# Four transposes in a row between two writes, and two neighbours exchanged on VectorE: a fused convolution and gated-MLP kernel

## The chip, the cores and the metric

The kernel runs on one core of a Trainium2 chip. The metric is the device time of one execution in microseconds (us). The kernel before took 234.76 us, the median of three runs (234.39 to 234.94). Besides these there is one profiled execution, from which all rows of the trace come; its own time is in the table below.

The engines are named as the profile names them: PE is TensorE (PEld its weight loads), DVE is VectorE, ACT is ScalarE, POOL is GpSimd, SP is SyncE. SP computes nothing; it issues DMAs, in order, and "SPq" is its queue.

## What is computed

Two branches work on the same normalised input and are added to it. Sequence length is 2048, width 640, inner width of the MLP 1728, all in bf16.

```python
x = A_q
xn = _layernorm(x, axis=-1)
return x + _A_ref(xn, A_k, A_v, A_shift_k, A_ssm_k, A_ssm_D) + _B_ref(xn, B_w_gate, B_w_up, B_w_down)
```

Branch A shifts `A_k` with four taps per channel, multiplies by `A_v` (the product is called kv), convolves kv along the sequence with the long filter `A_ssm_k` (by Fourier transforms of double length), adds `kv * ssm_D`, and multiplies by xn. Branch B is a gated MLP:

```python
g = jnp.einsum("bsd,df->bsf", x, w_gate)
u = jnp.einsum("bsd,df->bsf", x, w_up)
h = _sigmoid(g) * u
return jnp.einsum("bsf,fd->bsd", h, w_down)
```

## The kernel before, in words

**Tiling.** A sequence row r is held as r = 16 p + b: p is the partition (128 of them), b one of 16 blocks. Branch B works on four groups t = 0 to 3 of four blocks each, that is 512 rows; branch A on five chunks c = 0 to 4 of 128 channels.

**Branch B, for each group.** DVE computes the statistics of x and the normalised rows (ln_norms, L210 and L214; ln_xn, L227), POOL the reciprocal root (ln_pow, L222). The products need xn transposed. For group 0 PE does that. For groups 1 to 3 a transposing DMA per block does it, called a turn: xn_turn(g, i), L249, issued on SP's queue, 128 x 640 elements each. Then come 13 gate products and 13 up products of five matmuls each (gate_mm and up_mm, both L270) and one mixed product for the last 64 columns (both_mm, L291). ACT takes the sigmoid of a gate product out of PSUM (gate_ev, L279). DVE multiplies it with the up product (up_ev, L285), which frees that PSUM slot; this is called a gate product below. Then PE forms the down products (down_mm, L314), in two halves of the width, and DVE adds them to x (down_ev, L319); this is an eviction.

**Branch A, for each chunk.** DVE forms kv in 16 operations (kv_op, L347 to L356) and brings the filter into the same layout with 32x32 transposes (h_turn, L333). The Fourier transform is done in two stages of matmuls with a trip through DRAM between them. Stage 1 has eight groups (st1_mm, L373 and L375); each is copied out of PSUM (st1_ev, L231 on ACT, L234 where it is on DVE), and two copies at a time are written to DRAM (wr1(c, k), L391, 512 KB, issued on SP). rd2 (L408) reads them back reordered, st2_mm (L417) is stage 2, st2_ev copies it out, and prod multiplies with the filter's spectrum in two steps on DVE: a shuffle of 32 partitions (L430) and a product (L432). Two inverse stages follow (inv1_mm, L446; inv2_mm, L487), again with a write (wr2) and a read (rdb) between them. inv1_ev copies out of PSUM, inv2_q (L492) multiplies with xn, inv2_x (L497) adds to x.

**PSUM.** There are two pools. One, with two places, serves the stages of branch A; the other, with four, serves all products of branch B and inv2. A matmul that takes a place waits until the engine that last read it is done. The tile framework, not the kernel, hands out places, and sets all waits from the order in which the program issues its steps.

**Order.** The loops only fill lists: each kind of step has a letter and a list of its calls. A string, ORDER (L660 to L670), then names the next step to issue, letter by letter, for all engines at once. Within one engine the order of the letters is the order of execution; between engines only the waits count. The letters that the change touches: `e` is a turn, `w` a wr1, `u` an up_ev, both_mul or down_ev, `p` a prod, `H` an h_turn. The letters that stand near them: `g` a product of branch B on PE, `a` and `A` a group of stage 1 and its copy, `s` a gate_ev, `l` ln_norms or ln_xn, `P` ln_pow, `k` a kv_op.

**Around the first place of the change.** While PE still forms group 0's down products, interleaved with stage 1 of chunk 0, DVE normalises group 1. SP's queue has loaded chunk 1's filter and v. In the kernel before it then holds turn 0, turn 1, wr1(0, 0), wr1(0, 1), turn 2, turn 3 of group 1, and behind them the loads for chunk 2 (halo, taps, k), the other two writes of chunk 0 and the load of x's third group (L135). The first gate product of group 1 reads all four turned blocks.

**Around the other two.** Some 60 us later PE works on group 2's products and stage 1 of chunk 3, while DVE evicts the last down product of group 1 and runs ahead with chunk 4's kv and with prod of the groups of stage 2.

Of the kernel before, what the change touches and what calls it, by code (L numbers as in the profile page):

```python
# [57 lines left out]
def kernel(  # L58
# [600 lines left out]

    ORDER = """  # L660
    mmmZmmmmmmmmmTmmmmmmmggsguggsggsuukkgggssukkggukksukkkgsgukkgggsgukkkggsgsukkguHstggguHDmmmsukkkkggg
    ukgukgaAlugaAlPgaAlllueewgaAwlPgaAklleeHDkgaAugaAkKTwgaAukkKwgaAukkHgaAukkkggsgggnustgaukKKgghakAsul
    rwAsakggluglsaksAugHggkAVrubkkkBlswKBukgggaTVsgpkusukawgDkHPlngAaAaskgAKwAkukgskpbgtkBsllBugauAkgagp
    sAaguswVpakAguhkHHAgrgDkwcgVklguCkkraeCagAgkAbuBkuBkkggKgkbBKpggBaeualwukkggeIuurlTklAehrgwtVbBBggag
    kAagppswuAagkuaKswrgpAAkaHAskWgHupDgakuVsAggswucglJukkgkrCsbgpBugaBaAgAWkkgsbspugPkrBgwpgsRnFkukgprc
    wgCJusgbgusgpuBdBWppbqrgsdBlRuqgBcqlCggJbsggksuBupgllkBbBgrqkWBgeaaeAAuppwdgaduRegaIAgrugpaAqaeqggup
    AwcCqpJguugdbgFBgbBqqgugBppdcpWCuJqgrpsgqbgBsuwFgrgqsbuBgpBRsuWgpdcpqqdguJgqCsrrbFBgsgRbugBBpdrsppug
    cdCqugCqgbsgWBqpqggusrBRbpudgrgqWspBpBqcupdJsgCbgRBpgBqqguWgsppuqscCudgJsguqgqgRdWgoquuqoddRgggRqquq
# [37 lines left out]
```

## Time and profile before

| | |
|---|---|
| median of three runs | 234.76 us (234.39 to 234.94) |
| the profiled execution's own time | 235.41 us |
| its span, first to last instruction | 233.6 us |
| PE busy | 228.1 us |
| DVE busy | 203.8 us |
| ACT busy | 122.0 us |
| DMA | 56.79 MB, mean 243 GB/s |

How to read the rows: in a timeline a row has its start and duration in us from the span's start, the engine, the line of the kernel, the operation, what it writes and reads, and how many instructions are merged in it. A bracket at the end gives the idle time of the engine just before the row and what ended it. A row of SPq is the issue of a DMA, that is, the time in which the queue was occupied with it; its data moves later, and "DMA to landing" counts from the start of the issue to the moment when all data has arrived. The duration of a matmul's row is modelled and longer than the distance to the next one, as matmuls are pipelined. A row of the view by windows gives, for a stretch of time, its length, the busy time of PE, PEld, DVE, ACT and POOL, the TensorE clock that was granted (1.00 is full speed), and in the last two columns the busy share of the 16 DMA engines and the GB/s that they moved.

### The profile page before, as it was taken

How to read it: one execution, taken by the hardware profiler on the slowest of the kernel's cores; microseconds unless marked ns; L12 is line 12 of the kernel's file. 1: busy time of each engine (PE TensorE's matmuls, PEld its weight loads, DVE VectorE, ACT ScalarE, POOL GpSimd, SP SyncE). 2: the span in 40 equal slices, each digit the busy share in tenths (PEclk: the TensorE clock that was granted, in tenths of full speed). 3: DMA queues.
4: the chain of work that ended last, by engine and by line, in shares of the span. 5: the costliest groups of instructions: out<-in, count | busy, mean ns of one | idle time of the engine just before them, and what ended most of it. 6: DMA issues, size and time to landing. Idle time of an engine off the chain costs nothing.

```text
span 233.6 us, 5418 instructions
## 1 busy us (share of the span) xinstructions
PE 228.1 (98%) x2199; PEld 130.9 (56%) x2200; DVE 203.8 (87%) x359; ACT 122.0 (52%) x156; POOL 12.0 (5%) x24
## 2 busy tenths in 40 slices
PE   7999999998999999999999999999999999999995
PEld 2854446786454555677554444478653544446772
DVE  5446999889679999999999999997899999897773
ACT  2533222376264877766775837674556667762000
POOL 5210000021001100000011000000000000000000
PEclk9999999999999999999999999999999999999999
DMA  6999999999899899999999899589989999464874
GB/s 198 327 278 221 248 282 361 203 96 262 268 260 289 213 389 244 276 213 232 320 273 263 219 340 278 161 206 173 286 216 311 269 267 250 126 149 128 232 253 143
DMA packets 93803, 56.79 MB, mean 243 GB/s; under 512 B 50964, under 2 KB 87890, under 8 KB 93650
## 3 DMA queue, kind: packets, MB, share of 16 engines
q1 hardware_dynamic: 93346, 56.03, 92.4%
q10 hardware_dynamic: 432, 0.41, 0.6%
q8 instruction: 17, 0.28, 0.5%
q14 instruction: 8, 0.07, 0.1%
HBM read 36.12 MB, written 18.35 MB: 233 GB/s over the span
## 4 chain that ended last, share of the span: by engine, by line
PE 91%; DVE 6%; DMA 1%; POOL 0%; issue 0%; ACT 0%; DVEq 0%
PE pu L270 24%; PE pg L270 23%; PE pd L314 22%; PE psb L487 4%; PE ps L417 3%; PE ps L375 3%; PE ps L373 3%; PE psa L446 2%; PE idle L513 2%; PE pg L291 2%; DVE st L210 1%; DVE x L319 1%; DMA xnT<-xn 1%; PE pg L261 1%; PE pu L261 1%; PE pt L241 1%
## 5 line engine op out<-in xcount | busy, mean ns | idle before, releaser
L270 PEld LDWEIGHTS <-w 128*128 128x128 bf16 x500 | 46.6, 98 | 55.8 <-issue 5.9
L314 PE MATMUL pd<-wd,hT 128*128 128x320 bf16 (+2 forms) x447 | 66.1, 299 | 0.1
L270 PE MATMUL pg<-xnT,w 128*128 128x512 bf16 x250 | 62.2, 379 | 1.1 <-DMA xnT<-xn 1.1
L270 PE MATMUL pu<-xnT,w 128*128 128x512 bf16 x250 | 62.2, 379 | 0.3 <-DVE hT L285 0.3
L314 PEld LDWEIGHTS <-hT 128*128 128x128 bf16 x448 | 41.7, 98 | 18.1 <-issue 2.4
L279 ACT ACTIVATE sig<-pg 128x512 bf16<-128x512 f32 x52 | 31.1, 601 | 32.3 <-PE pg L270 26.9
L285 DVE TENSOR_TENSOR hT<-sig,pu 128x512 bf16<-128x512 bf16 x52 | 34.9, 678 | 10.5 <-PE pu L270 5.2
L231 ACT CAST xz<-ps 128x1024 bf16<-128x1024 f32 x36 | 35.1, 1015 | 15.8 <-PE ps L417 15.7
L231 ACT CAST t<-ps 128x1024 bf16<-128x1024 f32 x24 | 23.9, 1013 | 19.9 <-PE ps L375 16.7
L432 DVE TENSOR_TENSOR xz<-xz 128x2048 bf16<-128x2048 bf16 x20 | 24.4, 1220 | 0.2
L375 PE MATMUL ps<-kvh,S1t 128*128 128x128 bf16 x160 | 21.7, 220 | 0.0
L373 PE MATMUL ps<-kvh,S1t 128*128 128x128 bf16 x160 | 21.6, 218 | 0.0
L351 DVE TENSOR_TENSOR tmp<-kx,sc 128x1024 bf16<-128x1024 bf16 x30 | 20.5, 683 | 0.3
L353 DVE TENSOR_TENSOR acc<-acc,tmp 128x1024 bf16<-128x1024 bf16 x30 | 20.4, 681 | 0.3
L319 DVE TENSOR_TENSOR x<-pd,x 128x320 bf16<-128x320 f32 (+2 forms) x32 | 15.1, 479 | 4.3 <-PE pd L314 4.1
L373 PEld LDWEIGHTS <-S1t 128*128 128x128 bf16 x160 | 15.5, 97 | 2.7 <-DVE kvh L356 0.2
L375 PEld LDWEIGHTS <-S1t 128*128 128x128 bf16 x160 | 15.4, 96 | 2.5
L210 DVE BATCH_NORM_STATS2 st<-x 128x6 f32<-128x320 bf16 x32 | 13.9, 476 | 2.2 <-DMA x<-in_A_q_dram 2.2
L231 ACT CAST TBt<-ps 128x1024 bf16<-128x1024 f32 x14 | 13.9, 1013 | 2.9 <-PE ps L375 2.9
L492 DVE TENSOR_TENSOR yx<-psb,xn 128x512 bf16<-128x512 f32 x20 | 13.7, 686 | 1.4 <-PE psb L487 0.8
L430 DVE STREAM_SHUFFLE xz<-xz 128x512 f32<-128x512 f32 x20 | 14.5, 725 | 0.0
L231 ACT CAST ao<-psa 128x1024 bf16<-128x1024 f32 x9 | 9.0, 1013 | 8.3 <-PE psa L446 6.9
(53 smaller groups left out, 157.8 us busy)
## 6 DMA issues: line engine op xcount, KB each, us to landing
t<-d SPq DMA_DIRECT2D x15, 512.0 KB, 5.9
d<-t SPq DMA_DIRECT2D x13, 512.0 KB, 5.7
d<-TBt SPq DMA_DIRECT2D x7, 512.0 KB, 6.4
d<-ao SPq DMA_DIRECT2D x6, 512.0 KB, 4.7
bi<-d SPq DMA_DIRECT2D x6, 512.0 KB, 4.5
kvh<-in_A_v_dram SPq DMA_DIRECT2D x10, 256.0 KB, 6.3
hn<-in_A_ssm_k_dram SPq DMA_DIRECT2D x20, 128.0 KB, 7.2
S1t<-d SPq DMA_DIRECT2D x4, 512.0 KB, 7.0
```

Source lines behind the costliest of these rows:

```text
L210: nc.vector.bn_stats(st[:, i, SD * s2:SD * s2 + SD], x[:, b, s2 * 320:(s2 + 1) * 320])
L231: nc.scalar.copy(out=out, in_=in_)
L270: nc.tensor.matmul(pg[:, :], lhsT=w[:, c, u * UP + fc * P:u * UP + (fc + 1) * P], rhs=xnT[:, :, c, :], start=(c == 0), stop=(c == NC - 1))
L279: nc.scalar.activation(sig[fc][:, :], pgs[0, fc][:, :], ACT.Sigmoid)
L285: nc.vector.tensor_tensor(hT[:, fc, :], sig[fc][:, :], pgs[1, fc][:, :], ALU.mult)
L314: nc.tensor.matmul(pd[:, :], lhsT=hT[:, fc, bb * P:(bb + 1) * P], rhs=wd[:, fc, es], start=(fc == 0), stop=(fc == NFC - 1))
L319: nc.vector.tensor_tensor(x[:, 4 * t + bb, es], pds[bb, half][:, :], x[:, 4 * t + bb, es], ALU.add)
L351: nc.vector.tensor_tensor(d["tmp"][:, :, :], kx[:, lo + 3 - m:hi + 3 - m, :], sb(m), ALU.mult)
L353: nc.vector.tensor_tensor(d["acc"][:, :, :], d["acc"][:, :, :], d["tmp"][:, :, :], ALU.add)
L373: nc.tensor.matmul(ps[:, i, 0:P], lhsT=S1[:, h, b, :], rhs=cin[c]["kvh"][:, 0, b, :], start=True, stop=True)
L375: nc.tensor.matmul(ps[:, i, P:2 * P], lhsT=S1[:, h, b, :], rhs=hp[:, b // 2, b % 2, :], start=True, stop=True)
L432: nc.vector.tensor_tensor(z[:, 1:3, :, :], z[:, 0:1, :, :].to_broadcast((P, 2, 8, P)), z[:, 1:3, :, :], ALU.mult)
```

## The change

Only the order string differs. No step is added, removed or altered.

```diff
-    ukgukgaAlugaAlPgaAlllueewgaAwlPgaAklleeHDkgaAugaAkKTwgaAukkKwgaAukkHgaAukkkggsgggnustgaukKKgghakAsul
+    ukgukgaAlugaAwlPgaAlllueegaAlPgaAklleewHDkgaAugaAkKTwgaAukkKwgaAukkHgaAukkkggsgggnustgaukKKgghakAsul
...
-    kAagppswuAagkuaKswrgpAAkaHAskWgHupDgakuVsAggswucglJukkgkrCsbgpBugaBaAgAWkkgsbspugPkrBgwpgsRnFkukgprc
+    kAagpupswAagkuaKswrgpAAkaHAskWguHpDgakuVsAggswucglJukkgkrCsbgpBugaBaAgAWkkgsbspugPkrBgwpgsRnFkukgprc
```

Read engine by engine, it does this:

- On SP's queue, wr1(0, 0) moves ahead of turns 0 and 1 of group 1, and wr1(0, 1) behind turns 2 and 3. The queue then holds wr1(0, 0), turn 0, turn 1, turn 2, turn 3, wr1(0, 1). What stands before and behind these six is unchanged.
- On DVE, down_ev(1, 3, 1), the last eviction of group 1, moves ahead of prod(3, 0), the shuffle of stage 2's group 3.
- On DVE, up_ev(2, 1), the second gate product of group 2, moves ahead of h_turn(4, 1), the second 32x32 transpose of chunk 4's filter.
- The orders on PE, ACT and POOL are the same.

## The prediction, made before the result was known

> **What bounds the kernel now.** I began with the busy times and the chain of work that ended last.
>
> ```profile
> PE 228.1 (98%) x2199; PEld 130.9 (56%) x2200; DVE 203.8 (87%) x359; ACT 122.0 (52%) x156; POOL 12.0 (5%) x24
> PE 91%; DVE 6%; DMA 1%; POOL 0%; issue 0%; ACT 0%; DVEq 0%
> ```
>
> TensorE (PE) is the bound: 98% of the span, 91% of the chain. Order alone can only remove moments in which PE stands still. The list of waits names two behind the first microseconds; PE's timeline shows them in brackets. As the ends of matmul rows are modelled, I measure a stop from start to start. The undisturbed step from a stage-1 matmul to a product is 0.06 us:
>
> ```profile
> 119.08 0.22 PE L375 MATMUL ps<-kvh,S1t 128*128 128x128 bf16 x1
> 119.14 0.59 PE L270 MATMUL pg<-xnT,w 128*128 128x512 bf16 x2
> ```
>
> The first stop, at the first gate product of the second group, costs 58.22 - 56.89 - 0.06 = **1.27 us**:
>
> ```profile
> 56.89 0.22 PE L375 MATMUL ps<-kvh,S1t 128*128 128x128 bf16 x1
> 58.22 1.24 PE L270 MATMUL pg<-xnT,w 128*128 128x512 bf16 x5 [1.12 <-DMA xnT<-xn]
> ```
>
> The second, at up_mm(2,1), has no bracket and costs 0.21 - 0.06 = **0.15**:
>
> ```profile
> 117.40 0.22 PE L375 MATMUL ps<-kvh,S1t 128*128 128x128 bf16 x1
> 117.61 1.24 PE L270 MATMUL pu<-xnT,w 128*128 128x512 bf16 x5
> ```
>
> The third, at up_mm(2,3), costs 0.50 - 0.06 = **0.44**:
>
> ```profile
> 123.22 0.22 PE L375 MATMUL ps<-kvh,S1t 128*128 128x128 bf16 x1
> 123.72 1.24 PE L270 MATMUL pu<-xnT,w 128*128 128x512 bf16 x5 [0.27 <-DVE hT L285]
> ```
>
> Together 1.86 us: the most that this change can win, as it removes no work.
>
> The first stop is a wait for the last transpose of x's second group (xn_turn(1,3)). Those transposes are issued on SyncE's queue:
>
> ```profile
> 41.37 1.34 SPq L183 DMA_DIRECT2D kvh<-in_A_v_dram  x1
> 48.17 1.31 SPq L249 DMA_TRANSPOSE xnT<-xn  x1
> 49.60 2.21 SPq L249 DMA_TRANSPOSE xnT<-xn  x1
> 51.91 0.53 SPq L391 DMA_DIRECT2D d<-t  x1
> 52.54 0.37 SPq L391 DMA_DIRECT2D d<-t  x1
> 53.00 2.31 SPq L249 DMA_TRANSPOSE xnT<-xn  x1
> 55.41 1.24 SPq L249 DMA_TRANSPOSE xnT<-xn  x1
> 56.70 0.57 SPq L165 DMA_DIRECT2D kx<-in_A_k_dram  x1
> ```
>
> The queue stands from 42.71 (41.37 + 1.34) to 48.17, the first turn waiting for its xn. Then two turns, both writes of stage 1 (wr1) and two more turns fill it without a gap to 56.65. The last turn lands 2.7 us after its issue began, the row below, so at 58.11, and PE starts at 58.22.
>
> ```profile
> DMA to landing us min/median/max: 2.7/2.7/2.7
> ```
>
> The other two stops are PSUM slots that VectorE (DVE) frees too late:
>
> ```profile
> 116.46 0.72 DVE L430 STREAM_SHUFFLE xz<-xz 128x512 f32<-128x512 f32 x1
> 117.08 0.47 DVE L319 TENSOR_TENSOR x<-pd,x 128x320 bf16<-128x320 f32 x1
> 117.48 0.68 DVE L351 TENSOR_TENSOR tmp<-kx,sc 128x1024 bf16<-128x1024 bf16 x1
> ```
>
> The eviction (L319) ends at 117.55 and PE starts at 117.61.
>
> ```profile
> 122.01 1.09 DVE L333 STREAM_TRANSPOSE kvh<-hn 128x512 f32<-128x512 f32 x1
> 123.03 0.63 DVE L285 TENSOR_TENSOR hT<-sig,pu 128x512 bf16<-128x512 bf16 x1
> 123.60 0.72 DVE L430 STREAM_SHUFFLE xz<-xz 128x512 f32<-128x512 f32 x1
> ```
>
> The gate product (L285) ends at 123.66 and PE starts at 123.72. In both places the change exchanges just the first two of these three rows.
>
> **Part 1, the queue.** Nothing is added or removed: six DMAs change order. The first write needs the second eviction of stage 1:
>
> ```profile
> 45.92 1.01 ACT L231 CAST t<-ps 128x1024 bf16<-128x1024 f32 x1 [0.39 <-PE ps L375]
> ```
>
> That ends at 46.93, so the write issues at about 47.0 for some 0.5 us, inside the queue's standing time. The first two turns keep their places. The third and fourth need these rows of xn:
>
> ```profile
> 50.98 0.80 DVE L227 TENSOR_SCALAR xn<-x,mv,rstd 128x640 bf16<-128x640 bf16 x2 [0.59 <-POOL rstd L222]
> ```
>
> Both are ready by 51.78, the first of them earlier, so the third turn starts at 51.87 instead of 53.00. With the four durations of the rows (1.31, 2.21, 2.31, 1.24) the last one is issued by 55.52 and lands, at 58.11 - 56.65 = 1.46 after its issue, at 56.98; with 1.3 for the third, which then has only a turn ahead of it, at 55.97. PE needs it by about 56.84. So the first stop goes, or all but about 0.15: I take 1.2 of the 1.27; the bounds are 1.27 and, by the second rival below, a loss.
>
> Behind them the second write goes out at 55.57 instead of 52.54. Its landing took 4.1 us there, and its buffer is filled again by chunk 1's third eviction:
>
> ```profile
> DMA to landing us min/median/max: 4.1/4.1/4.1
> ```
> ```profile
> 65.39 1.01 ACT L231 CAST t<-ps 128x1024 bf16<-128x1024 f32 x1 [2.60 <-issue]
> ```
>
> That would be 59.7 against 64.1 (65.39 less the 1.27): nobody waits. If the cover went, ACT would wait, and PE for its bank. The next load (chunk 2's halo, 56.70) then starts at 56.15, 0.55 us sooner, or up to 2.0 sooner if all turns take 1.25.
>
> **Part 2, what is late next.** PE alone being early isn't enough, since its PSUM slots come from DVE, and DVE waits for loads:
>
> ```profile
> 67.79 0.89 DVE L210 BATCH_NORM_STATS2 st<-x 128x6 f32<-128x320 bf16 x2 [0.16 <-DMA x<-in_A_q_dram]
> ```
> ```profile
> 78.59 0.63 DVE L285 TENSOR_TENSOR hT<-sig,pu 128x512 bf16<-128x512 bf16 x1
> ```
> ```profile
> 79.30 1.24 PE L270 MATMUL pu<-xnT,w 128*128 128x512 bf16 x5
> ```
>
> From 67.79 on DVE runs practically without a gap, and its start there is pinned by the load of x's third group. At 79.30 PE takes a slot that DVE freed at 79.22. So behind this point PE keeps only as much of its gain as DVE has moved, and DVE moves only as much as that load lands sooner. How much is that? The DMA engines by windows:
>
> ```profile
> 51.00:52.00 1.00, 1.00 (x14) 0.82 (x12) 1.00 (x3) 0.61 (x2) 0.00 (x0) 1.00 0.06 6
> 54.00:55.00 1.00, 1.00 (x13) 0.77 (x11) 1.00 (x3) 0.66 (x1) 0.00 (x0) 1.00 1.03 397
> 56.00:57.00 1.00, 1.00 (x13) 0.78 (x11) 1.00 (x3) 0.80 (x1) 0.00 (x0) 1.00 1.01 207
> 57.00:60.00 3.00, 1.88 (x11) 0.86 (x10) 2.93 (x6) 1.51 (x2) 0.00 (x0) 1.00 0.54 124
> ```
>
> The last two columns are DMA share and GB/s. From 57 to 60 they are idle for 0.46 of 3 us, 1.4 us, because the queue hands out too little; another 0.94 us is lost at 51, while the queue still issues turn 1 and next to nothing moves. With the queue ahead by 0.55 to 2.0 us and a write (512 KB, 1.3 us at 397 GB/s) to fill the hole at 57, the load lands sooner by between 0.55 (the issue alone) and about 1.9 (nearly all idle time used). I take **1.0**, nearer the lower end, as the row that is sure is the issue's. So of the first stop 1.0 us survives at 79.30.
>
> **Part 3, the exchanges on DVE.** At 117 the eviction no longer stands behind the shuffle (0.62 us from start to start), at 123 the product no longer behind the 32x32 transpose (1.02). Both stops, 0.15 and 0.44, are shorter, so both go. What moves back, a shuffle by 0.40 us (117.48 less 117.08, the eviction's step) and a 32x32 transpose by 0.57, costs nothing by these rows: behind each pair every row of DVE starts when it did, and the shuffle's reader and chunk 4's h are wanted only there or later. If PE took its slot from DVE without a stop here, the exchanges would be worth nothing. PE would then be 1.0 + 0.59 us ahead, DVE only 1.0, and DVE gets no faster. The tightest later place is this one:
>
> ```profile
> 149.65 1.22 DVE L234 CAST ao<-psa 128x1024 bf16<-128x1024 f32 x1
> ```
> ```profile
> 151.13 0.43 PE L417 MATMUL ps<-t,SMt 32*32 32x512 bf16 x16
> ```
>
> PE takes the bank at 151.13 and DVE left it at 150.87. The slack is 0.26, less the 0.06 of every hand-over, so 0.2 of the lead on DVE can be kept: 1.0 + 0.2 = **1.2 us** in all. Behind that DVE is the one that waits for PE, as in this row, so the lead stays to the end.
>
> ```profile
> 159.69 1.22 DVE L234 CAST t<-ps 128x1024 bf16<-128x1024 f32 x1 [1.24 <-PE ps L375]
> ```
>
> The sum: the profiled execution took 235.41 us (span 233.6 and 1.8 around it), 0.65 above the median of the runs, and becomes 234.2. The median, 234.76, becomes **233.5**.
>
> One page can be held against the way I priced the turns. In the window at 56, which holds little but two turns, the engines move 207 GB/s, against 397 at 54, where the write moves. The Trainium skill (Advanced Engine Details and Errata, X-Bar Transpose) says that transposing DMAs on trn2 are as fast as regular ones, at an expected 350 to 400 GB/s. The trace disagrees by nearly a factor of two. By the page a turn's 164 KB would take an estimated 0.41 us, and the sum would be that of the fourth rival below.
>
> **The rivals.**
> - *DVE stays where it is.* If the load of x lands no sooner, DVE is pinned at 67.79, PE is stopped at 79.30 for what it won at 58, and only the 0.2 us of slack at 151 is left from the exchanges, with 0.05 from 79.30. For it: at 54 and 56 the share is 1.0, so what lands late may be set by the engines and not by the issue. Against it: the 1.4 us of idle time just before. 234.76 - 0.25 = **234.5**.
> - *The turns pace each other: slower.* Turn 1, right behind turn 0, took 2.21 us to issue; turn 3, right behind turn 2, only 1.24. If a turn in a row costs 2.3, four end at 48.17 + 9.2 + 0.15 = 57.5, the last lands at 59.0 (PE +0.9), and the halo starts at 58.15 instead of 56.70. The load of x and with it DVE are 1.4 late, PE at 79.30 too; 0.2 comes back from the exchanges: 234.76 + 1.2 = **236.0**. It decides from a mean of 1.93 us a turn, at which the halo keeps its 56.70; in the rows the mean is 1.77. Against it: the long ones also had a stalled engine or two writes ahead of them.
> - *The exchanges do nothing.* Which of four PSUM slots a product gets is the tile framework's choice in program order, and with the order changed it may pick another. Then 0.2 is lost: **233.7**.
> - *The turns run at the rate of a plain write.* With four issues of 1.25 the halo goes out at 54.65, DVE moves by all that PE feeds it (1.27, and the 0.16 it waited at 67.79), and PE keeps 1.43 + 0.2: 234.76 - 1.63 = **233.1**. For it: the two short rows. Against it: the 207 GB/s.
>
> **How the numbers follow.** The forecast gets 0.59, the plain-write rival 0.08, the idle exchanges 0.10, the pinned DVE 0.13, the pacing turns 0.10. A measurement can tell 0.2%, 0.47 us, from no change. Faster by more than that are the first three, 0.77; the same is the pinned DVE, 0.13; slower the pacing turns, 0.10. The range goes from all three stops gone (234.76 - 1.86 = 232.9) to just above the pinned DVE (234.6) and leaves out the slower rival.
>
> **What would show it.** Right: the first write issued at about 47; the four turns end by 55.6; PE goes from 56.95 into the first product of the second group; no step above 0.06 near 116 and 122; the load of x lands about 1 us sooner, and so does DVE's first statistics row behind it. Wrong: turns of over 1.93 us each; a new wait of PE for DVE near 78, or near 150 of more than I allow; a transpose landing still named ahead of the first gate product. If the load of x lands no sooner, part 2 has failed; if PE still steps by 0.2 or 0.5 at 116 and 122, part 3 has.

## The result, and the profile after

The changed kernel took **233.73 us** (median of six runs, 233.54 to 234.25) against 234.92 us for the kernel before (six runs, 234.39 to 235.34): a ratio of 0.9954, interval 0.9939 to 0.9970. Two further sets of runs gave 0.9943 (0.9916 to 0.9970) and 0.9930 (0.9896 to 0.9963); the profiled execution of the first of them, at 599 us, was a disturbed one and isn't used. The forecast was 233.5 us in a range of 232.9 to 234.6, with faster as the likeliest. The profiled execution took 233.65 us, with a span of 231.9 instead of 233.6.

The page of the changed kernel, busy times and chain:

```profile
PE 227.8 (98%) x2199; PEld 131.2 (57%) x2200; DVE 203.4 (88%) x359; ACT 122.0 (53%) x156; POOL 12.0 (5%) x24
PE 98%; DVE 0%; issue 0%
```

No work has gone: PE and DVE are as busy as before. But the chain is PE's alone, 98% instead of 91%; DVE's 6% and the DMA's 1% are no longer links in it. PE's list of waits has one row left, from the first microseconds:

```profile
PE idle L513 <- DVE st L123: 1.2, 1, 1.2
```

The three places at which PE stopped, in PE's timeline of the changed kernel (start, duration; look at the distance from start to start):

```profile
56.98 0.22 PE L375 MATMUL ps<-kvh,S1t 128*128 128x128 bf16 x1
57.04 0.38 PE L270 MATMUL pg<-xnT,w 128*128 128x512 bf16 x1
...
116.23 0.22 PE L375 MATMUL ps<-kvh,S1t 128*128 128x128 bf16 x1
116.29 0.38 PE L270 MATMUL pu<-xnT,w 128*128 128x512 bf16 x1
...
121.91 0.22 PE L375 MATMUL ps<-kvh,S1t 128*128 128x128 bf16 x1
121.96 0.38 PE L270 MATMUL pu<-xnT,w 128*128 128x512 bf16 x1
```

All three steps are 0.05 or 0.06 us, the undisturbed one: 1.27, 0.15 and 0.44 are gone. SP's queue shows why at the first:

```profile
47.05 0.34 SPq L391 DMA_DIRECT2D d<-t  x1
48.19 1.31 SPq L249 DMA_TRANSPOSE xnT<-xn  x1
49.59 2.30 SPq L249 DMA_TRANSPOSE xnT<-xn  x1
51.98 1.23 SPq L249 DMA_TRANSPOSE xnT<-xn  x1
53.31 1.23 SPq L249 DMA_TRANSPOSE xnT<-xn  x1
54.63 0.54 SPq L391 DMA_DIRECT2D d<-t  x1
55.23 0.41 SPq L165 DMA_DIRECT2D kx<-in_A_k_dram  x1
...
59.16 0.49 SPq L135 DMA_DIRECT2D x<-in_A_q_dram  x1
```

The first write sits in the queue's standing time. The last turn is issued by 54.54, 2.11 us earlier than before (56.65): 1.00 for the two writes that no longer stand between, and most of the rest because turn 2 took 1.23 us instead of 2.31. It lands at 53.31 + 2.6 = 55.9, 1.1 us ahead of PE:

```profile
DMA to landing us min/median/max: 2.6/2.6/2.6
```

And DVE, whose lead the forecast worried about:

```profile
65.76 0.69 DVE L285 TENSOR_TENSOR hT<-sig,pu 128x512 bf16<-128x512 bf16 x1 [1.68 <-ACT sig L279]
66.36 0.49 DVE L210 BATCH_NORM_STATS2 st<-x 128x6 f32<-128x320 bf16 x1
...
148.02 1.22 DVE L234 CAST ao<-psa 128x1024 bf16<-128x1024 f32 x1
```

The statistics row starts at 66.36 instead of 67.79, and has no wait for the load of x any more (issued 59.16, landed 6.4 us later, at 65.52). What holds DVE here is PE's product, by way of ACT's sigmoid, in the row above it. At 148.02, against 149.65, DVE is 1.63 us ahead.

### The profile page after: what moved, and what is told of

The parts are those of the page before. It is cut to its first block, busy times and chain, and to the rows that moved or that the text cites. A ratio compares the mean times of both kernels' runs of the same rounds, so it can differ in the third digit from the quotient of the medians.

```text
span 231.9 us, 5417 instructions
## 1 busy us (share of the span) xinstructions
PE 227.8 (98%) x2199; PEld 131.2 (57%) x2200; DVE 203.4 (88%) x359; ACT 122.0 (53%) x156; POOL 12.0 (5%) x24
## 4 chain that ended last, share of the span: by engine, by line
PE 98%; DVE 0%; issue 0%
PE pd L314 27%; PE pu L270 24%; PE pg L270 24%; PE psb L487 4%; PE ps L375 4%; PE ps L373 4%; PE ps L417 3%; PE psa L446 3%; PE idle L513 2%; PE pg L291 2%; PE pg L261 1%; PE pu L261 1%; PE pt L241 1%; DVE x L319 0%; DVE hT L119 0%
```

## The experiments

**How they are read.** A stop is the step from start to start less 0.06, as in the prediction. "DVE ahead" is 149.65 less the start of the copy L234 near there; "PE ahead" is 151.50 (where the first down product of the third group stood before) less its start. Each execution also has its own offset of up to 0.6 us, in one case 2 us, mostly from its first 45 us, where the loads land differently each time; it is in both columns alike, so their difference is the sound number. The diffs below are against the changed kernel and show only the part of the string that differs.

| kernel | ratio (interval) | span | stop at 57 | at 117 | at 123 | DVE ahead | PE ahead |
|---|---|---|---|---|---|---|---|
| before | 1 | 233.6 | 1.27 | 0.15 | 0.44 | 0 | 0 |
| before_again | 1.0014 (0.9991 to 1.0037) | 236.2 | 1.52 | 0.19 | 0.43 | -2.57 | -2.57 |
| before_look | one run, 235.37 us | 233.6 | 0.97 | 0 | 0.24 | 0.03 | 0.03 |
| changed | 0.9954 (0.9939 to 0.9970) | 231.9 | 0 | 0 | 0 | 1.63 | 1.76 |
| after_again | 0.9943 (0.9916 to 0.9970) | | | | | | |
| after_look | 0.9930 (0.9896 to 0.9963) | 231.8 | 0 | 0 | 0 | 1.71 | 1.82 |
| turns_only | 0.9961 (0.9935 to 0.9986) | 232.1 | 0 | 0 | 0.24 | 1.54 | 1.54 |
| dve_only | 0.9997 (0.9965 to 1.0029) | 234.0 | 1.54 | 0 | 0 | -0.63 | -0.41 |
| x_late | 1.0021 (0.9994 to 1.0047) | 234.1 | 0 | 0 | 0 | -0.70 | -0.48 |
| writes_first | 0.9963 (0.9941 to 0.9985) | 233.3 | 0.89 | 0 | 0 | 0.07 | 0.28 |
| turns_first | 0.9976 (0.9953 to 0.9999) | 232.3 | 0 | 0 | 0 | 1.08 | 1.29 |
| write0_ahead | 0.9942 (0.9917 to 0.9968) | 231.5 | 0 | 0 | 0 | 2.05 | 2.16 |
| write1_behind | 0.9948 (0.9915 to 0.9980) | 232.8 | 0 | 0 | 0 | 0.60 | 0.82 |
| split_writes | 0.9962 (0.9937 to 0.9988) | 232.3 | 0.73 | 0 | 0 | 1.20 | 1.30 |

Ratios whose intervals overlap are not told apart by time; the conclusions below rest on the traces, and on ratios only where it is said.

**before_again and before_look: how much do the stops vary?** No edit.

> The kernel before, unchanged, profiled once more. In the prediction's trace the first stop of PE (ahead of the first gate product of group 1) was 1.27 us, and that execution was 0.65 us above its median. If the stop varies from run to run with the landing of the loads that stand ahead of the turns, it should be shorter here, about 0.7 us, with the stops at 117 and 123 unchanged (0.15 and 0.44); if it is fixed by the issue of the queue, it is again 1.2 to 1.3 us. Time: the same as before, ratio 1.000 within 0.001.

> The kernel before, one more profiled execution, to see how the stop at the second group's first product varies. In the three executions of this queue order so far it was 1.27, 1.52 and 1.54 us. Expected: between 1.0 and 1.6, the turn behind the two writes takes 2.1 to 2.4 us to issue, and the steps at up_mm(2,1) and up_mm(2,3) are 0.15 and 0.44 within 0.05. If the profiled execution was a bad one, the stop at the first product is below 0.8, which would explain why the medians differ by 1.2 us and the two profiled executions by 1.75.

In before_look PE's timeline has

```profile
57.50 0.22 PE L375 MATMUL ps<-kvh,S1t 128*128 128x128 bf16 x1
58.53 0.38 PE L270 MATMUL pg<-xnT,w 128*128 128x512 bf16 x1 [0.81 <-DVE acc L353]
...
123.39 0.22 PE L375 MATMUL ps<-kvh,S1t 128*128 128x128 bf16 x1
123.69 0.38 PE L270 MATMUL pu<-xnT,w 128*128 128x512 bf16 x1
```

The stop at 57 is 0.97 here, so it neither went below 0.8 nor stayed within 1.0 to 1.6, and 1.52 in before_again, above both values that were expected there. (The bracket names a DVE row, but the last turn landed at 58.39; a wait for several things is put down to one of them. In all six executions that stop here, before, before_again, before_look, dve_only, writes_first and split_writes, the product starts 0.13 or 0.14 us after that landing.) The three stops add up to 1.86, 2.14 and 1.21 us in three executions of the same kernel. In the one whose first stop was short, the others were too: DVE, relative to PE, was further ahead. Its first statistics row of x's third group starts 9.35 us after PE's first product of the second group there, against 9.57 and 9.76 in the other two; in turns_only, with the same 0 and 0.24, it is 9.32. So the expectation that the other two are fixed at 0.15 and 0.44 was wrong.

**after_again and after_look: is the gain one lucky execution?** No edit.

> The changed kernel, unchanged, profiled once more on this chip. Theory (all three stops gone, DVE ahead by more than PE): 1.1 to 1.3 us below before, no stop over 0.06 us on PE between 57 and 158, the last turn landing about 1 us ahead of its use. Rival (part of the gain in the first trace was luck of that execution): a stop of PE of 0.3 us or more somewhere between 57 and 158.

> The changed kernel once more, for a second profiled execution and its ratio. Expected: no step of PE above 0.06 us beyond the undisturbed one between 57 and 158 us, turns 2 and 3 at 1.2 to 1.35 us of issue each, ratio 0.993 to 0.996. If the profiled gain of 1.75 was one lucky execution, stops come back at 57 or 123 and the ratio is nearer to 0.997.

It isn't: no stop in after_look either, turns 2 and 3 at 1.23 us each, and both ratios near the expected band or at its lower end.

**turns_only and dve_only: the two halves.** turns_only has the queue's new order and DVE's old one:

```diff
-    kAagpupswAagkuaKswrgpAAkaHAskWguHpDgaku
+    kAagppswuAagkuaKswrgpAAkaHAskWgHupDgaku
```

> Only the queue's part of the change: the four turns in a row between the two writes, DVE in the order of before. Theory: DVE gains more than PE from the queue (its start on x's third group moved by 1.4 us against 1.2 for PE), so it no longer is late at the other two places: the stop at 117 vanishes, that at 123 shrinks from 0.44 to about 0.1, and nearly the whole gain is there, within 0.15 us of the full change. Rival (the parts add): the stops of 0.15 and 0.44 stay, and this is 0.5 to 0.6 us slower than the full change.

dve_only has DVE's new order and the queue's old one:

```diff
-    ukgukgaAlugaAwlPgaAlllueegaAlPgaAklleewHDk
+    ukgukgaAlugaAlPgaAlllueewgaAwlPgaAklleeHDk
```

> Only the two exchanges on DVE, the queue in the order of before. Theory (DVE gets no faster, so PE may keep only its slack on DVE further on, tightest 0.2 us at the bank of stage 2 near 151): the stops at 117 and 123 go, but new ones appear behind them, and 0.2 to 0.3 us is left. Rival (the parts add): 0.5 to 0.6 us faster than before, no new stop.

PE in turns_only, at the third place (the second has the undisturbed 0.06):

```profile
121.88 0.22 PE L375 MATMUL ps<-kvh,S1t 128*128 128x128 bf16 x1
122.18 0.38 PE L270 MATMUL pu<-xnT,w 128*128 128x512 bf16 x1
```

The queue alone removes the second stop and leaves 0.24 of the third, since it moved DVE by more than PE: 1.46 us at the load of x (66.33 against 67.79), PE 1.21 at the first product (57.01 against 58.22). The whole change is 0.2 us better in span: between the theory's 0.15 and the rival's 0.5, nearer the theory, though 0.1 was expected of the third stop. (The medians, 234.11 and 233.64, differ by 0.47, as the rival had it; but the intervals of their ratios overlap widely, and PE's records show the 0.24 and nothing else.) PE in dve_only:

```profile
57.36 0.22 PE L375 MATMUL ps<-kvh,S1t 128*128 128x128 bf16 x1
58.96 0.38 PE L270 MATMUL pg<-xnT,w 128*128 128x512 bf16 x1 [1.38 <-DMA xnT<-xn]
...
151.48 0.50 PE L417 MATMUL ps<-t,SMt 32*32 32x512 bf16 x16
151.91 0.31 PE L314 MATMUL pd<-wd,hT 128*128 128x320 bf16 x1
```

From the first product (58.96, before 58.22: 0.74 late) to the down product (151.91, before 151.50: 0.41 late) it wins 0.33 of the 0.59, and the rest comes back as new small stops near 131 and at 151, where the step from L417 is 0.43 instead of 0.37. That is about the theory's 0.2 to 0.3, and the new stops are what the rival excluded. The time can't decide it: 0.9997, with an interval that holds both.

**x_late: does DVE's lead decide?** The load of x's third group goes two places later, behind the rest of chunk 2's k and chunk 3's halo:

```diff
-    HgaAukkkggsgggnustgaukKKgghakAsul
+    HgaAukkkggsgggustgaukKKngghakAsul
```

> The changed kernel, with the load of x's third group issued two places later on SP's queue, behind the second half of chunk 2's k and chunk 3's halo. In the changed kernel it is issued at 59.16 and lands at 65.56, and DVE begins ln_norms(2,0) at 66.36. Theory (DVE's lead decides what PE may keep): the load is issued at about 62.4 and lands at about 67.6, DVE begins there some 1.3 us later than in the changed kernel, its lead over the kernel before falls from 1.54 to about 0.25, PE stops at up_mm(1,8) (78.1) for about 0.8 and near 131 or 151 again, and of the 1.75 us of span won 0.4 to 0.6 are left: about 1.2 us slower than the changed kernel. Rival (DVE is fed by PE's products there and the load has room): less than 0.2 us slower than the changed kernel, no new stop at 78.

DVE and PE in this kernel:

```profile
68.68 0.49 DVE L210 BATCH_NORM_STATS2 st<-x 128x6 f32<-128x320 bf16 x1 [2.44 <-DMA x<-in_A_q_dram]
```
```profile
78.95 0.22 PE L375 MATMUL ps<-kvh,S1t 128*128 128x128 bf16 x1
80.05 0.38 PE L270 MATMUL pu<-xnT,w 128*128 128x512 bf16 x1 [0.89 <-DVE hT L285]
```

DVE waits for the load, 2.3 us later than in the changed kernel, and PE gives back 1.04 us at up_mm(1,8), the place that the prediction named, after 0.42 and 0.41 at two products ahead of it. The four turns are still in a row, nothing stops at 57, 117 or 123, and yet the whole gain is gone: 1.0021. This is the theory, with a bigger price than expected: DVE lost 2.3 us, not 1.3, and nothing is left of the gain, where 0.4 to 0.6 was expected.

**writes_first: both writes ahead of the turns.**

```diff
-    gaAwlPgaAlllueegaAlPgaAklleewHDk
+    gaAwlPgaAlllugaAweelPgaAklleeHDk
```

> The changed kernel, with the second write ahead of the four turns as well: wr1(0,0), wr1(0,1), turn 0, 1, 2, 3. The turns begin at about 50.2 instead of 48.19, 2.0 us later. Theory (a turn behind a turn costs 1.25 us of the queue, and turn 1's 2.30 in the changed kernel was the stall beside the instruction fetch at 49.5, when turn 0 was in flight; here no turn is in flight then): four turns end by about 55.4, the last lands at about 56.8, PE passes into the second group's first product at about 57.0, and the time is that of the changed kernel within 0.3 us. Rival (turns in a row pace each other at 1.6 us on average, as the four of the changed kernel did): they end at 56.6, the last lands at 58.0, PE stops for 1.0 us at 57 and the gain falls to about 0.7.

```profile
50.27 2.17 SPq L249 DMA_TRANSPOSE xnT<-xn  x1
...
52.54 1.22 SPq L249 DMA_TRANSPOSE xnT<-xn  x1
```
```profile
56.95 0.22 PE L375 MATMUL ps<-kvh,S1t 128*128 128x128 bf16 x1
57.90 0.38 PE L270 MATMUL pg<-xnT,w 128*128 128x512 bf16 x1 [0.73 <-DVE acc L353]
```

The stop of 0.89 is nearly the rival's size, but not for its reason: turns 1 to 3 took 1.22 or 1.23 each, so a turn doesn't pace the next. Turn 0, directly behind the second write and with both still on their way (they landed at 51.23 and 53.23), took 2.17. The theory was right on the turns in a row, and had missed that the cost moves to the turn that follows the writes.

**write0_ahead and write1_behind: either write alone.**

```diff
-    gaAwlPgaAlllueegaAlPgaAklleewHDk
+    gaAwlPgaAlllueegaAwlPgaAklleeHDk
```

> Between the two kernels: the first write ahead of the turns, the second still between the two pairs: wr1(0,0), turn 0, 1, wr1(0,1), turn 2, 3. Theory (a write between turns costs the queue more than its own 0.5 us of issue, since the turn behind it takes 2.2 to 2.3 us to issue instead of 1.25): turn 2 ends at about 54.7, turn 3 at 56.0, the last lands at about 57.4 and PE still stops for about 0.4 us at 57; of the 1.27 us two thirds are won. Rival (a write costs its 0.5 us and no more): turn 3 ends at about 55.0 and lands at 56.4, PE doesn't stop, and the time is that of the changed kernel within 0.2 us.

```diff
-    gaAwlPgaAlllueegaAlPgaAklleewHDk
+    gaAlPgaAlllueewgaAlPgaAklleewHDk
```

> The other half of the queue's change: the second write behind the four turns, the first one still between the two pairs: turn 0, 1, wr1(0,0), turn 2, 3, wr1(0,1). With the first write alone ahead, the run before this one had no stop at 57. Theory (it is the pair of writes in a row ahead of a turn that costs: 1.0 us of issue and 0.9 to 1.0 more in the turn behind it; one write costs 0.5 and some 0.25): turn 2 starts at about 52.4, takes about 1.5 us to issue, turn 3 ends at about 55.2 and lands at about 56.6, PE doesn't stop, and the time is that of the changed kernel within 0.3 us, ratio 0.993 to 0.996. Rival (the first write has to be issued in the queue's standing time): turn 2 takes 2.2 us again, the last turn lands at about 57.3, PE stops for 0.4 us and the ratio is 0.996 to 0.998.

In write0_ahead turn 2 and turn 3:

```profile
51.37 1.47 SPq L249 DMA_TRANSPOSE xnT<-xn  x1
...
52.93 1.24 SPq L249 DMA_TRANSPOSE xnT<-xn  x1
```

In write1_behind turn 2, and PE at the first product:

```profile
52.45 1.46 SPq L249 DMA_TRANSPOSE xnT<-xn  x1
```
```profile
57.07 0.22 PE L375 MATMUL ps<-kvh,S1t 128*128 128x128 bf16 x1
57.13 0.38 PE L270 MATMUL pg<-xnT,w 128*128 128x512 bf16 x1
```

Neither stops. With one write between the pairs, turn 2 takes 1.47 or 1.46, not 2.2, and the last turn lands in time. The theory of write0_ahead fell, and its rival's time held (0.9942, against 0.9943 for the changed kernel in its second set of runs); for write1_behind the theory held. So half of the queue's change does all of it. (write1_behind's PE is only 0.82 ahead at 151 since it lost 0.85 us from 127 on, where a copy on DVE waited 0.82 us for a transfer of branch A; no other profiled execution has that wait, and I can't say what caused it.)

**split_writes: one write behind each of turn 0 and turn 2.**

```diff
-    gaAwlPgaAlllueegaAlPgaAklleewHDk
+    gaAlPgaAllluewegaAlPgaAklleweHDk
```

> Both writes stay between the turns, but not in a row: turn 0, wr1(0,0), turn 1, turn 2, wr1(0,1), turn 3. Theory (two writes in a row ahead of a turn are what costs): turn 1 and turn 3, each behind one write, take at most 1.6 us to issue; the last turn is issued by about 55.3, lands at about 56.7, and PE doesn't stop at 57 or for 0.1 us at most: the time is that of the changed kernel within 0.3 us. Rival (the 1 MB of the two writes costs the queue 2.0 us wherever it stands among the turns): the last turn is issued by about 56.5, lands at about 57.9, PE stops for 1.0 us, and the gain is about 0.7.

```profile
50.03 1.97 SPq L249 DMA_TRANSPOSE xnT<-xn  x1
...
54.04 1.51 SPq L249 DMA_TRANSPOSE xnT<-xn  x1
```
```profile
56.71 0.22 PE L375 MATMUL ps<-kvh,S1t 128*128 128x128 bf16 x1
57.50 0.38 PE L270 MATMUL pg<-xnT,w 128*128 128x512 bf16 x1 [0.57 <-DMA xnT<-xn]
```
```profile
DMA to landing us min/median/max: 3.3/3.3/3.3
```

Between the two: the queue is done by 55.55, 1.1 us sooner than before, as the theory had it to 0.25 us, but the last turn lands 3.3 us after the start of its issue instead of 2.6. The stop is 0.73, so the theory's time failed. (Turn 1, behind one write too, took 1.97: it ran in the hole that the last section describes.) What counts is the landing of the last turn, and what goes out directly ahead of it delays that landing beyond its issue. In write1_behind the last turn starts at 53.99, behind a turn, and lands at 56.64; here it starts at 54.04, behind a write, and lands at 57.37.

**turns_first: the first write behind the turns too.**

```diff
-    gaAwlPgaAlllueegaAlPgaAklleewHDk
+    gaAlPgaAlllueegaAlPgaAklleewwHDk
```

> The changed kernel, with the first write behind the turns as well: turn 0, 1, 2, 3, wr1(0,0), wr1(0,1). Theory (what counts is that no write stands between the turns; the first write's own place has room): the turns keep their times, the last lands at about 55.9, the first write goes out at about 54.6 and lands at about 57.6, so that chunk 1's first eviction on ACT (55.88) waits 1.7 us, which PE doesn't feel, as the gate product behind it is wanted only at 61; the time is that of the changed kernel within 0.3 us. Rival (the write has to use the queue's standing time): ACT's wait reaches PE's PSUM places, a stop of 0.5 to 1.5 us between 58 and 64, and that much of the gain is lost.

```profile
57.52 1.93 ACT L231 CAST t<-ps 128x1024 bf16<-128x1024 f32 x2 [1.81 <-PE ps L375]
```
```profile
66.88 0.49 DVE L210 BATCH_NORM_STATS2 st<-x 128x6 f32<-128x320 bf16 x1 [0.17 <-DMA x<-in_A_q_dram]
```

ACT's copy starts at 57.52 instead of 55.88, when the write has landed (57.42), and PE doesn't feel it: no stop between 57 and 123. So the standing time wasn't needed for that. But with one more write ahead of them all loads behind go out later, x lands at 66.86 instead of 65.52, DVE is pinned by it again, and PE gives back 0.2 at 131 and 151: small, and again through DVE. The span is 0.4 longer than the changed kernel's, about half of it this execution's offset, and the intervals of the ratios overlap; so the theory's 0.3 is neither confirmed nor refuted by the time.

## Why the prediction was right, point by point

- **The first write in the standing time.** Right: 47.05, predicted about 47.0. But not needed for the gain: with either write alone out of the way there is no stop (write0_ahead, write1_behind), and none with both behind the turns (turns_first).
- **The turns.** The prediction gave two ends for the last landing, 56.98 if turn 2 keeps its 2.31 us of issue, and 55.97 if it falls to 1.3. It fell to 1.23, and the landing is 55.9. The runs show the reason that the prediction only surmised: of the second group's turns, one behind two writes in a row takes 2.15 to 2.31 (five executions, writes_first among them), behind one write 1.46 to 1.51 (three; a fourth, turn 1 of split_writes, took 1.97 in the hole of the last section), behind a turn 1.20 to 1.35 outside that hole. A turn that starts 0.5 to 0.8 us after a write's issue has ended takes 1.30 to 1.35 (turn 0 in changed, after_look, turns_only, x_late and write0_ahead), hardly more than with no write ahead of it (1.30 or 1.31), so in the standing time the write costs the turns next to nothing.
- **The first stop.** 1.27 gone, 1.2 predicted.
- **The load of x and DVE's move: this step failed in size.** Predicted: the load sooner by 0.55 to 1.9, and so DVE by 1.0, "nearer the lower end, as the row that is sure is the issue's". Measured: the halo issued 1.47 us sooner (55.23 against 56.70), the load landed 2.2 sooner (65.52, against 67.76), DVE 1.43 sooner at 66.36 and 1.63 at 148. The 2.2 lie beyond the bound of 1.9: the load was issued 1.24 sooner (59.16 against 60.40) and then took 6.4 us to land instead of 7.4. I had assumed that DVE stays pinned by the load; it came off it and was then fed by PE. That the load is what can pin it is shown by x_late and turns_first.
- **The two exchanges.** Right that both stops go and that what moves back costs nothing: no new stop shows in the changed kernel. But they are not worth 0.59 each time. Once the queue had moved DVE by more than PE, the second stop was gone without its exchange, and the third was 0.24 (turns_only).
- **The cap of 0.2 behind 150.** Right in size, without effect here. In the four kernels in which DVE was the limit (dve_only, x_late, writes_first, turns_first), and in write1_behind after its own stop, PE's lead ends 0.21 or 0.22 above DVE's, whatever that was. In the changed kernel it is 0.13 above, so the cap doesn't bind and the 1.86 is kept (1.76, as this execution comes to the first place 0.09 later). The prediction had not seen that part of this lead is given back at 131 already.
- **The sum.** For the profiled execution it said 1.2 and 234.2 us; measured were 1.76 and 233.65. The sum was 0.55 short, as DVE's move had been put 0.63 too low. The median came out at 1.2 all the same (234.92 - 233.73), partly since the kernel before varies: the 1.86 is that of the execution from which the sum was made, and another of the three had 1.21. The other two sets give 1.3 us (0.57% of 235.6) and 1.6 (0.70% of 235.36). So the gain lies at 1.2 to 1.6 us, and the forecast at the lower end of it. That it met the first median to 0.2 us is partly luck: DVE's move was put too low, and the stops were those of an execution in which they were longer than in another.
- **The rivals.** The pinned DVE is no story of this kernel, but it is exactly what x_late made of it. The idle exchanges gave 233.7, which is the median that was measured, but not for their reason: the third stop, 0.24 in turns_only, goes with its exchange, and dve_only wins 0.33 with the exchanges alone. The pacing turns fell with turns 2 and 3 at 1.23 and with writes_first. The plain-write rival named the right move of DVE (all that PE feeds it, 1.43 at the load of x, as measured) for a wrong reason: the turns in a row kept to 1.23 us of the queue each and didn't move at a write's rate. On the Trainium skill's transposes at the speed of regular DMAs (Advanced Engine Details and Errata, X-Bar Transpose), the trace disagrees further: 164 KB in 1.33 us from issue to issue is 123 GB/s, a pace that the issue sets.

## What to carry to other kernels

When a transfer that somebody waits for lands depends on what stands ahead of it in the issuing queue: here two 512 KB writes cost their 1.0 us of issue and another 0.9 to 1.1 in the transpose behind them, while one cost 0.5 and 0.25, and the landing came later still behind a write (3.3 to 3.4 us from the start of the issue, against 2.6 to 2.8 behind a transpose, both outside the hole of the next section). A stop removed on the bounding engine is kept only as far as the engine that feeds it has moved too, so look for the wait that pins that engine (here a load 10 us later) and see how near it is to binding. And stops that look independent may hang on the same lead: add them up only after asking what the first one's removal does to the others.

## What the hardware showed that was not expected

While turn 0 was in flight, hardly any data moved for about a microsecond (6 GB/s from 50.5 to 51.5), though the engines count as busy: the share above 1 in the first row is that of packets which began there and lasted into the next. In the kernel before, the row at 50 has a share of 2.11, so the 0.94 us that the prediction called lost at 51 was such time too, and not time in which the engines had nothing to do. The windows of the changed kernel (DMA share and GB/s in the last two columns):

```profile
50.00:51.00 1.00, 1.00 (x12) 0.73 (x10) 0.47 (x1) 0.78 (x1) 0.99 (x1) 1.00 1.69 28
51.00:52.00 1.00, 1.00 (x15) 0.85 (x13) 0.93 (x3) 0.61 (x2) 0.03 (x1) 1.00 0.26 46
```

From 49 to 52 the DMA view has one packet in the instruction queue, which I take for a fetch of instructions:

```profile
q8 instruction: 1, 0.02, 2.6%
```

The ten profiled executions in which that fetch, at 49.3 to 50.4, found a turn in flight have such a hole and a long turn 1 (1.48 to 2.30 us of issue, in x_late 1.22 and then a gap), and turn 0 lands 4.0 to 4.9 us after the start of its issue. In before_again, dve_only and writes_first no turn was in flight at the fetch; turn 0 lands after 2.7 us in the first two, and after 3.9 behind the writes of writes_first. That the fetch causes the hole is argued from this, not shown: no kernel moved the fetch alone. It isn't what made the first stop, which was longest (1.52 and 1.54) in two executions without it.

That the issue of a turn grows with what is ahead of it fits what the Trainium skill says of the recorded time (Perfetto Trace Analysis, DMA Instruction — HWDGE (DVE, Sync)): it covers the wait until the descriptor generator is free and the generating, while the moving of the data is not in it, though it may begin before the generating has ended. The trace agrees on the last point as far as it goes: turn 3 of the changed kernel was issued by 54.54 and landed 1.36 us later. For the growth it has the durations alone, 1.23 us behind a turn and 2.15 to 2.31 behind two writes; whether a full descriptor buffer holds the second up no run here shows.
